# A fused attention and two-layer kernel: the first batch's w1/w2 products ordered by feature tile, its softmax weights transposed by products with a diagonal of reciprocal sums, and more filling products at the start

## The chip, the cores and the metric

The kernel runs as one program on one core of a Trainium2 chip. The metric is the device time of one execution in microseconds (us); a lower number is better. TensorE (called PE in the profile, its weight loads PEld) multiplies, VectorE (DVE) and ScalarE (ACT) do the elementwise work, GpSimd (POOL) issues the loads and stores, and SyncE (SP) issues the transposing transfers of the attention weights.

## The reference, cut to what matters

```python
def _attn_ref(q, k, v):                       # (4, 8, 576, 64), block-causal, block of 64
    scores = scale * np.matmul(q, k.transpose(0, 1, 3, 2))
    scores = np.where(mask, scores, -1000000000.0)
    scores = scores - np.max(scores, axis=-1, keepdims=True)
    attn = np.exp(scores)
    attn = attn / (np.sum(attn, axis=-1, keepdims=True) + 1e-09)
    return np.matmul(attn, v)

def _moe_ref(x, w1, w2, w3, w_out):           # x: 2304 x 512, w1, w2: 512 x 1024
    a = x @ w1
    b = x @ w2
    h = a * b @ w3
    return h @ w_out

def _moe2_ref(x, w_in, w_out):                # 512 -> 2048 -> 512
    h = x @ w_in
    r = np.maximum(h, 0.0)
    return (r * r) @ w_out
```

The attention of 4 batches with 8 heads gives the 2304 x 512 matrix x of the first layer, whose result is the x of the second. The weights come as 64-bit floating-point words.

## The kernel before, in words

**Attention.** The 32 heads are handled as 16 pairs p; pairs 0 to 3 are batch 0, pairs 4 to 7 batch 1, and so on. The 576 queries of a head are cut into five tiles, in three groups g. For each pair and group PE makes the scores `s`, DVE takes the maxima `nm`, ACT makes the exponentials `pf` and their sums `ssum`, and DVE makes the reciprocals `r`. Batch 0 then goes its own way (`whole(p)`): DVE multiplies each row of `pf` by its reciprocal (L842), PE transposes `pf` with the identity `ident` into PSUM (`transpose`, tile `tp`, L900), ACT copies that to `pt` (L906), and PE multiplies `pt` by the values (`attend_whole`, L1003). A group has five transpositions for each of the two heads, so a pair has 30 and the four pairs 120. From batch 1 on ACT and DVE write f16 high and low parts `p`, a DMA transposes them, and PE makes the value products at L949. The result x of a pair is kept as f16 high and low parts in two token parts, x0 (320 tokens) and x1 (256 tokens); g = 0 and g = 1 of the first layer are these two parts.

**Weights.** `w3 @ w_out` is computed once, by the products `po` of `setup_rows` (L1040, evicted by ACT at L1116 and by DVE at L1121). The eight tiles of w1 and w2 (one for 128 features, f = 0 to 7) are converted by `w12_tile`: a load, two passes of ACT and two of DVE, a sum of squares or a maximum, a small product with ones on PE (L351, `wsum`), a scale, and a split into f16 high parts (ACT, L278) and low parts (DVE, L281).

**First layer.** `first_block(b, g)` runs over the eight features f and the two halves `which` (0 for w1, 1 for w2): twelve products `ab` into a PSUM bank, then an eviction by ACT (`a`), a product of both halves by DVE (L1184) and a split into high and low parts of the tile `g`. After all eight features come the products `y` with `w3 @ w_out`, stored to DRAM. The calls for g = 0 and g = 1 follow each other, so that g = 0 wants all eight converted tiles before anything of g = 1 is done. Everything else of PE after that, the rest of the batches and the second layer, follows in the same manner.

**What sets the order.** The program is written as operations with inputs, outputs, an assumed cost and a key; `Order.emit` puts them into each engine's queue: whenever an engine is free in its model, the ready operation with the lowest key comes next. Engines run their queues in order. The keys around the change are these:

```python
key = 2 * p * HEAD + 5 * g          # scores of pair p, group g (HEAD = 10); + 3 behind the softmax
key = (2 * p + 1) * HEAD + 6 + part # value products of pair p
K12 + K12S * (n - 13)               # the 16 half tiles of w1/w2: 60, 62, ... 90 before
```

The products `po`, `ab` and `y` have keys far above these, in the order in which they are written, so they fill PE whenever no attention is ready. For pairs from 4 on, `spare(p)` adds a reserve (2.0 us in the model) before PE's score and value products are thought ready. `Order.idle` calls `warm_up` while the first weights are still on their way: wherever PE would sit idle, it writes filling products `warm_out` (128 columns, bf16) that nobody reads; `begin_warm` and `end_warm` bound that time.

Of the kernel before, what the change touches and what calls it, by code (L numbers as in the profile page):

```python
# [7 lines left out]
F32 = mybir.dt.float32  # L8
# [162 lines left out]
def fused_kernel(ctx: ExitStack, tc: tile.TileContext, qT, kT, vp, va, w12, w3t, wo, wb, out):  # L171
# [45 lines left out]
    GATE_A = 1  # L217
    GATE_G = 1
    KWO, KWOS, KW3, KW3S = 0,3,14,4
    K12 = 60.0  # L220
    K12S = 2.0
    VSL = 7
    LOADL = 2
    VSB = 4.2
# [1 line left out]
    X0KEY = 2.0  # L226

    SPARE = 2.0
    S_SPARE = 0.7


# [261 lines left out]

    def spare(p):

        return SPARE if p >= KDM else 0.0

    raws = {}
    vals = {}
# [18 lines left out]
    table = buf("at", "table", 1, [P, 1], F32, "table")  # L518
    warm_out = buf("p0", "po", 1, [P, 512], F32, "warm_out")

    def warm_up(gap):
        for _ in range(int((0.8 * gap - 0.2) / 0.11)):
            pe.matmul(warm_out()[:, :P], warm(), warm(), start=True, stop=True)

    def begin_warm():
# [199 lines left out]
    def pair(p):  # L725
# [6 lines left out]
        for g, ts_ in enumerate(GROUPS):  # L732
# [101 lines left out]

            od.op(DVE, 0.17, reciprocals, [(ssum, k, a) for k in range(nt) for a in range(2)], [(r,)], key)
            blocks = sum(2 * t + 1 for t in ts_)
            for a in range(2):
                if whole(p):
                    for k, t in enumerate(ts_):
                        od.op(  # L840
                            DVE, 0.12 + 0.0006 * n_keys(t),
                            lambda a=a, k=k, w=weights, r=r: dve.tensor_scalar(  # L842
                                out=w(a, k), in0=w(a, k), scalar1=r()[:, k, a : a + 1], scalar2=None, op0=ALU.mult
                            ),
                            [(r,)], [(pfs[a], k)], key,
                        )
                    transpose(p, g, a, pfs[a], weights, key)
                    continue
                pt = pts[2 * p + a, g] = at_buf(f"pt{g}{a}", 1, [P, blocks, P], F16, f"pt_{name}_{a}")
                pts_of[pt] = 2 * p + a, g  # L850
                p16 = at_buf("p16", P_BUFS, [P, 9 * P], F16, f"p16_{name}_{a}")
                for k, t in enumerate(ts_):
                    nk = n_keys(t)
                    o = PT_BASE[t] * P
                    od.op(
                        ACT, c_act(nk, 0.09),
                        lambda o=o, nk=nk, a=a, k=k, w=weights, p16=p16, r=r: act.activation(  # L857
                            p16()[:, o : o + nk], w(a, k), AF.Copy, scale=r()[:, k, a : a + 1]
                        ),
                        [(pfs[a], k), (r,)], [(p16, "h", t)], key,  # L860
                    )
                    od.op(
                        DVE, c_dve(nk, 0.06),
                        lambda o=o, nk=nk, a=a, k=k, w=weights, p16=p16, r=r: dve.scalar_tensor_tensor(  # L864
                            out=p16()[:, o + nk : o + 2 * nk], in0=w(a, k), scalar=r()[:, k, a : a + 1],
                            in1=p16()[:, o : o + nk], op0=ALU.mult, op1=ALU.subtract,
                        ),
                        [(pfs[a], k), (r,), (p16, "h", t)], [(p16, "l", t)], key,
                    )
                whole_p = [(p16, x, t) for x in "hl" for t in ts_]  # L870
                pt_keys[2 * p + a, g] = [(pt,)]
                od.op(
                    SQ, (1.25, 0.22 * blocks, LATE),
                    lambda p16=p16, pt=pt, blocks=blocks: sp.dma_start_transpose(
                        out=pt(), in_=p16()[:, : blocks * P]
                    ),
                    whole_p, [(pt,), ("pt", 2 * p + a, g)], key,
                )
# [1 line left out]

    WHOLE_PT = {1: (0, 3), 2: (1, 4), 3: (0, 3), 0: (3, 4), 4: (0, 4)}

    def transpose(p, g, a, pf, weights, key):

        ts_ = GROUPS[g]
        name = f"{p}_{g}_{a}"
# [4 lines left out]
        for part, (todo, n) in enumerate(((mains, P), (lasts, 64))):  # L891
# [4 lines left out]
            def go(todo=todo, n=n, tp=tp, first=first):  # L896
                for k, c, o in todo:
                    nq = 64 if ts_[k] == 0 else P
                    at = (o - first) * P
                    pe.transpose(tp()[:n, at : at + nq], weights(a, k)[:nq, c * P : c * P + n], ident()[:nq, :nq])  # L900

            od.op(PE, len(todo) * 0.12 + 0.05, go, [(pf, k) for k in range(len(ts_))] + [(ident,)], [(tp,)], key)
            last = ("pt", 2 * p + a, g)
            od.op(
                ACT, c_act(wide),
# [233 lines left out]

    last_y = []  # L1140

    def first_block(b, g):
        gt0, gn = GS[g]
        x = xs[b, g]
        gs = []
        gt = {}
        for f in range(KFF):
            accs = []
            for which in range(2):
                acc = Acc(gn, f"ab_{b}_{g}_{f}_{which}")  # L1150
                mms = []
                for kc in range(KDM):
                    for a, xn in PRODS:
                        o = which * 512 + kc * P
                        mms.append((
                            lambda a=a, xn=xn, o=o, kc=kc, f=f: (w12_view(f, a)[:, o : o + P], x[xn][kc]()),
                            [w12_key(f, a, which), (x[xn][kc],)],
                        ))
                accumulate(acc, mms, gn, next_key(), c_mm16)
                accs.append(acc)  # L1160
                back = Part(ab_back[b], 2 * f + which, 1)
                if which == 0:
                    av = buf("mo1", "a", 2, [P, GMAX], F32, f"a_{b}_{g}_{f}")
                    od.op(
                        ACT, c_act(gn, 0.09),
                        lambda av=av, acc=acc, back=back: act.activation(av()[:, :gn], acc(), AF.Copy, scale=back()),
                        [acc.key, (ab_back[b], f)], [(av,)], K_EVICT,
                    )
                else:
                    if f % 4 == 0:  # L1170
                        gt[f // 4] = g_buf(f // 4, f"g_{b}_{g}_{f}")
                    t = gt[f // 4]
                    o = 2 * (f % 4)

                    def hi(t=t, o=o):
                        return t()[:, o * GMAX : o * GMAX + gn]

                    def lo(t=t, o=o):
                        return t()[:, (o + 1) * GMAX : (o + 1) * GMAX + gn]

                    kh, kl = (t, "h", f % 4), (t, "l", f % 4)
                    od.op(
                        DVE, c_dve(gn, 0.06),
                        lambda acc=acc, av=av, back=back: dve.scalar_tensor_tensor(  # L1184
                            out=av()[:, :gn], in0=acc(), scalar=back(), in1=av()[:, :gn], op0=ALU.mult, op1=ALU.mult
                        ),
                        [acc.key, (ab_back[b], f)], [(av,)], K_EVICT,
                    )
                    split(hi, lo, lambda av=av: av()[:, :gn], gn, ([kh], [kl], (av,)), K_EVICT)
                    gs.append(((hi, lo), (kh, kl)))  # L1190

        def ys_products(key=None):
            for e in range(KDM):
# [680 lines left out]
    for b in range(B):  # L1874
# [22 lines left out]
            begin_blocks()  # L1897
        else:
            ab_scales(b)
        for g in range(2):  # L1900
            first_block(b, g)
    second_block()
    od.emit()

# [50 lines left out]
```

## Time and profile before

| | |
|---|---|
| median of 3 runs | 885.81 us (885.78 to 887.76) |
| profiled execution | 883.62 us, of which the span of its instructions is 881.5 us |
| PE busy in the span | 850.7 us (97%), 7143 products |
| DVE, ACT, POOL busy | 632.6 us (72%), 571.7 us (65%), 107.9 us (12%) |
| mean granted TensorE clock | 0.988 of full speed |

The profile is one execution. Times in its rows are microseconds from the start of the span; an engine's idle time in a stretch is the stretch less its busy time. The granted clock has two levels here, 1.2 and 2.4 GHz, shown as 0.5 and 1.0 of full speed.

### The profile page before, as it was taken

The numbers are of one execution on the slowest core, as the hardware profiler recorded it, in microseconds if no ns is written. First come the engines' busy times: TensorE is split into PE (matmuls) and PEld (weight loads), VectorE is DVE, ScalarE is ACT, GpSimd is POOL, SyncE is SP. The second block draws the span as 40 slices with busy tenths as digits, with TensorE's granted clock in tenths as the row PEclk, the third lists the DMA queues.
The fourth block names the chain that finished last, engine by engine and source line by source line (L and its number), as shares of the span: only waits on it lengthen the run. The fifth ranks groups of instructions, "written<-read, shape, count | busy, mean of one in ns | idle before, by whom it ended". The sixth has DMA issues, their size and how long they took to land.

```text
span 881.5 us, 18383 instructions
## 1 busy us (share of the span) xinstructions
PE 850.7 (97%) x7143; PEld 643.7 (73%) x7147; DVE 632.6 (72%) x1470; ACT 571.7 (65%) x1304; POOL 107.9 (12%) x202
## 2 busy tenths in 40 slices
PE   7799988899999999999999999999999999999998
PEld 6477875588877888779979877666666666666664
DVE  5987979888778787763993788997853474375443
ACT  5987878677766676774895696664544464464343
POOL 5111112020121101002221111000010000000000
PEclk8999998899999999999999999999999999999999
DMA  8833348589998999883563342000020002001001
GB/s 312 321 123 104 122 147 231 125 149 185 183 196 158 184 167 177 155 136 111 195 204 119 105 143 73 1 25 1 2 97 1 1 29 67 1 1 48 1 1 48
DMA packets 104247, 98.06 MB, mean 111 GB/s; under 512 B 82976, under 2 KB 86816, under 8 KB 102752
## 3 DMA queue, kind: packets, MB, share of 16 engines
q0 software_dynamic: 17568, 69.09, 24.6%
q1 hardware_dynamic: 86592, 27.80, 18.9%
q8 instruction: 56, 0.92, 0.4%
q14 instruction: 31, 0.25, 0.1%
HBM read 60.69 MB, written 9.44 MB: 80 GB/s over the span
## 4 chain that ended last, share of the span: by engine, by line
PE 59%; DVE 3%; ACT 1%; issue 0%; DVEq 0%
PE o L1785 20%; PE p L1721 16%; PE ab L1040 11%; PE y L1040 7%; PE h L1636 2%; PE pv_bank L949 1%; PE s L757 1%; PE ny L1343 0%; DVE s L1663 0%; DVE nm L791 0%; DVE g L271 0%; DVE ob L1795 0%; DVE c L1742 0%; DVE p L864 0%; PE nq L1464 0%
## 5 line engine op out<-in xcount | busy, mean ns | idle before, releaser
L1785 PE MATMUL o<-wb,g 128*128 128x512 f16 x864 | 194.5, 379 | 0.1
L1040 PEld LDWEIGHTS <-w 128*128 128x128 f16 x1536 | 147.8, 99 | 51.8 <-ACT w L278 4.7
L1785 PEld LDWEIGHTS <-g 128*128 128x128 f16 x864 | 84.0, 98 | 92.4 <-issue 0.6
L1040 PE MATMUL ab<-x0h,w 128*128 128x320 f16 x512 | 112.8, 307 | 6.8 <-ACT w L278 3.1
L1040 PE MATMUL y<-g,w3o 128*128 128x320 f32 (+1 forms) x768 | 110.1, 299 | 0.5 <-DVE g L242 0.5
L816 ACT ACTIVATE pf<-s,nm 128x192 f32<-128x192 f32 (+4 forms) x160 | 82.9, 527 | 39.6 <-DVE nm L799 39.5
L1040 PEld LDWEIGHTS y<-g,w3o 128*128 128x128 f32 x768 | 103.6, 188 | 3.8 <-issue 1.9
L1609 ACT ACTIVATE c<-c,beta 128x512 f32<-128x512 f32 x64 | 45.4, 713 | 81.5 <-DVE c L1742 81.4
L1040 PE MATMUL ab<-x1h,w 128*128 128x256 f16 x512 | 87.9, 273 | 0.5 <-DVE a L1184 0.5
L1721 PEld LDWEIGHTS <-wb 128*128 128x128 f16 x768 | 75.2, 98 | 15.8 <-issue 0.2
L271 DVE TENSOR_TENSOR g<-c,g 128x512 f16<-128x512 f32 x64 | 43.7, 689 | 48.8 <-ACT g L269 48.8
L1040 PE MATMUL ab<-x0l,w 128*128 128x320 f16 x256 | 78.4, 306 | 0.0
L864 DVE SCALAR_TENSOR_TENSOR p<-pf,r,p 128x192 f16<-128x192 f32 (+2 forms) x120 | 62.6, 546 | 16.4 <-ACT p L857 15.7
L1040 PE MATMUL ab<-x1l,w 128*128 128x256 f16 x256 | 69.8, 272 | 0.0
L857 ACT ACTIVATE p<-pf,r 128x192 f16<-128x192 f32 (+2 forms) x120 | 60.8, 559 | 5.0 <-ACT pf L816 1.6
L1040 PE MATMUL po<-wo,w 128*128 128x256 f32 (+1 forms) x360 | 55.5, 303 | 8.6 <-DVE w3o L1121 4.8
L1721 PEld LDWEIGHTS <-st 128*128 128x128 f16 x576 | 56.4, 98 | 7.4
L1742 DVE TENSOR_TENSOR c<-p,x 128x512 f32<-128x512 f32 x32 | 22.1, 690 | 50.9 <-PE p L1721 40.2
L1040 PEld LDWEIGHTS po<-wo,w 128*128 128x128 f32 x360 | 47.1, 195 | 14.0 <-DVE w3o L1121 3.9
L757 PE MATMUL s<-kraw,qraw 64*128 64x288 f32 (+4 forms) x384 | 54.5, 409 | 1.2 <-ACT pf L816 1.2
L332 DVE CUSTOM_DVE_ANT_0 cx<-raw,cx 128x1024 uint16<-128x1024 uint16 (+1 forms) x61 | 47.6, 781 | 2.9 <-ACT raw L323 0.4
L319 ACT ACTIVATE raw<-raw 128x512 f32<-128x512 f32 (+1 forms) x61 | 46.4, 763 | 1.6 <-DMA raw<-in_w 1.4
(213 smaller groups left out, 1645.6 us busy)
## 6 DMA issues: line engine op xcount, KB each, us to landing
raw<-in_wb POOLq DMA_DIRECT2D x32, 512.0 KB, 4.9
raw<-in_w3t POOLq DMA_DIRECT2D x8, 1024.0 KB, 12.6
raw<-in_w POOLq DMA_DIRECT2D x16, 512.0 KB, 5.0
vraw<-in_vp POOLq DMA_DIRECT2D x16, 320.0 KB, 4.9
qraw<-in_qT POOLq DMA_DIRECT2D x16, 288.0 KB, 4.1
kraw<-in_kT POOLq DMA_DIRECT2D x32, 144.0 KB, 4.3
yraw<-ydram POOLq DMA_DIRECT2D x8, 512.0 KB, 4.7
vmix<-v SPq DMA_DIRECT2D x24, 160.0 KB, 4.4
```

The lines of the kernel that those rows point to most:

```text
L271: DVE, c_dve(n), lambda: dve.tensor_tensor(out=lo(), in0=src(), in1=hi(), op=ALU.subtract), kh + ks, kl, key
L319: act.activation(up, up, AF.Prelu, scale=2.0**-112, alpha=2.0**32)
L332: dve.tensor_tensor(out=x(), in0=x(), in1=words()[1], op=ALU.add)
L757: pe.matmul(o[:, h] if t == 4 else o, q()[rows, q_start(t) : q_start(t) + 128], keys_()[rows, c], start=True, stop=True,)
L816: act.activation(o, view(a, t), AF.Exp, bias=nm()[:, k, a : a + 1], scale=SCALE, accum_out=ssum()[:, k, a : a + 1],)
L857: lambda o=o, nk=nk, a=a, k=k, w=weights, p16=p16, r=r: act.activation(p16()[:, o : o + nk], w(a, k), AF.Copy, scale=r()[:, k, a : a + 1]),
L864: lambda o=o, nk=nk, a=a, k=k, w=weights, p16=p16, r=r: dve.scalar_tensor_tensor(out=p16()[:, o + nk : o + 2 * nk], in0=w(a, k), scalar=r( ...
L1040: pe.matmul(acc(), l, r, start=k == 0, stop=k == len(mms) - 1)
L1609: lambda: act.activation(src(), src(), AF.Relu, scale=beta()[:, j, k : k + 1]),
L1721: pe.matmul(acc()[:, TH * half : TH * half + TH], lhs(a, kc), y[yn]()[:, kc], start=n == 0, stop=n == len(mms) - 1,)
L1742: DVE, c_dve(n), lambda: dve.tensor_tensor(out=o(), in0=x(), in1=y(), op=ALU.add), r, w, K_EVICT
L1785: pe.matmul(o(), g[gx]()[:, cols], wt(f)[:, a, 512:1024], start=(begin and n == 0), stop=(last and n == 2),)
```

## The change

Four things are changed.

1. For batch 0 the first layer goes feature tile by feature tile: for each f the products of both token parts, and the products `y` only after all eight. Token part 1 gets `g` tiles of its own (`w8_0`, `w8_1`, where the converted w_out was). The other batches keep their order.
2. In batch 0 the rows of `pf` are no longer multiplied by the reciprocals. DVE makes for each group a tile `dg` of diagonal matrices, the identity times the reciprocals, one for each tile and head, and the transposition becomes an ordinary F32 product of `pf` with its diagonal matrix. The costs that the planner assumes for it are unchanged.
3. The conversions of w1 and w2 get the keys 50, 54, ... 110, and the reserve of pairs 4 to 7 falls from 2.0 to 1.0.
4. `warm_up` counts 0.062 instead of 0.11 us for a filling product after its first use, so that a gap of the same length gets more of them (170 in all instead of 114).

```diff
-    K12 = 60.0
-    K12S = 2.0
+    K12 = 50.0
+    K12S = 4.0
...
+    SPARE_1 = 1.0
...
-        return SPARE if p >= KDM else 0.0
+        return 0.0 if p < KDM else SPARE_1 if p < 2 * KDM else SPARE
...
+    warm_cost = [0.11]
+
     def warm_up(gap):
-        for _ in range(int((0.8 * gap - 0.2) / 0.11)):
+        n = int((0.8 * gap - 0.2) / warm_cost[0])
+        if n > 0:
+            warm_cost[0] = 0.062
+        for _ in range(n):
             pe.matmul(warm_out()[:, :P], warm(), warm(), start=True, stop=True)
...
+            if whole(p):
+                dg = at_buf("dg", 2, [P, 4, P], F32, f"dg_{name}")
+                od.op(
+                    DVE, c_dve(2 * nt * P),
+                    lambda nt=nt, dg=dg, r=r: dve.tensor_tensor(
+                        out=dg()[:, : 2 * nt], in0=ident().unsqueeze(1).broadcast_to([P, 2 * nt, P]),
+                        in1=r().rearrange("p k a -> p (k a)")[:, : 2 * nt].unsqueeze(2).broadcast_to([P, 2 * nt, P]),
+                        op=ALU.mult,
+                    ),
+                    [(r,), (ident,)], [(dg,)], key,
+                )
             for a in range(2):
                 if whole(p):
-                    for k, t in enumerate(ts_):
-                        od.op(
-                            DVE, 0.12 + 0.0006 * n_keys(t),
-                            lambda a=a, k=k, w=weights, r=r: dve.tensor_scalar(
-                                out=w(a, k), in0=w(a, k), scalar1=r()[:, k, a : a + 1], scalar2=None, op0=ALU.mult
-                            ),
-                            [(r,)], [(pfs[a], k)], key,
-                        )
-                    transpose(p, g, a, pfs[a], weights, key)
+                    transpose(p, g, a, pfs[a], weights, dg, key)
...
-                    pe.transpose(tp()[:n, at : at + nq], weights(a, k)[:nq, c * P : c * P + n], ident()[:nq, :nq])
-
-            od.op(PE, len(todo) * 0.12 + 0.05, go, [(pf, k) for k in range(len(ts_))] + [(ident,)], [(tp,)], key)
+                    pe.matmul(
+                        tp()[:n, at : at + nq], weights(a, k)[:nq, c * P : c * P + n], dg()[:nq, 2 * k + a, :nq],
+                        start=True, stop=True,
+                    )
+
+            od.op(PE, len(todo) * 0.12 + 0.05, go, [(pf, k) for k in range(len(ts_))] + [(dg,)], [(tp,)], key)
...
+    def first_block(b):
+        gs = [Products() for _ in GS]
+        if b:
+            for g in range(2):
+                for f in range(KFF):
+                    ab_products(b, g, f, gs[g])
+                y_products(b, g, gs[g])
+            return
+        for f in range(KFF):
+            for g in range(2):
+                ab_products(b, g, f, gs[g])
+        for g in range(2):
+            y_products(b, g, gs[g])
```

The first place is DVE behind the reciprocals `r` of pair 1, group 1 (the names carry pair, group and head). Before:

```order
L829 TENSOR_SCALAR r_1_1_657<-ssum_1_1_617 128x4
L833 RECIPROCAL r_1_1_657<-r_1_1_657 128x4
L842 TENSOR_SCALAR pf_1_1_0_616<-pf_1_1_0_616,r_1_1_657 128x448
L1121 TENSOR_TENSOR w3o_0_532<-po_405,w3o_0_532 128x256
L842 TENSOR_SCALAR pf_1_1_0_616<-pf_1_1_0_616,r_1_1_657 128x64
L842 TENSOR_SCALAR pf_1_1_1_647<-pf_1_1_1_647,r_1_1_657 128x448
L242 TENSOR_TENSOR w3_3_661<-cx_9_600,w3_3_661 128x1024
L842 TENSOR_SCALAR pf_1_1_1_647<-pf_1_1_1_647,r_1_1_657 128x64
```

With the change:

```order
L835 TENSOR_SCALAR r_1_1_685<-ssum_1_1_637 128x4
L839 RECIPROCAL r_1_1_685<-r_1_1_685 128x4
L847 TENSOR_TENSOR dg_1_1_694<-ident_92,r_1_1_685 128x512
L330 TENSOR_SCALAR cx_9_697<-raw_9_200 128x1024
L780 MEMSET s_1_2_0_688 64x64
```

Four passes over `pf` have become one over `dg`, and both heads' products wait for that one.

The second place is PE at the transpositions of pair 1, group 0, with the products `po` between the two heads. Before:

```order
L900 MATMUL tp_1_0_0_0_595<-ident_92,pf_1_0_0_538 128x128 x3
L900 MATMUL tp_1_0_0_1_603<-ident_92,pf_1_0_0_538 64x128 x2
L1040 MATMUL po_405<-wo_1_417,w3_1_535 128x256 x6
L900 MATMUL tp_1_0_1_0_619<-ident_92,pf_1_0_1_545 128x128 x3
L900 MATMUL tp_1_0_1_1_623<-ident_92,pf_1_0_1_545 64x128 x2
```

With the change:

```order
L909 MATMUL tp_1_0_0_0_599<-dg_1_0_594,pf_1_0_0_558 128x128 x3
L909 MATMUL tp_1_0_0_1_604<-dg_1_0_594,pf_1_0_0_558 64x128 x2
L1052 MATMUL po_459<-wo_0_307,w3_1_587 128x256 x6
L1052 MATMUL po_459<-wo_1_468,w3_1_587 128x256 x6
L1052 MATMUL po_459<-wo_2_522,w3_1_587 128x256 x6
L909 MATMUL tp_1_0_1_0_639<-dg_1_0_594,pf_1_0_1_583 128x128 x3
L909 MATMUL tp_1_0_1_1_646<-dg_1_0_594,pf_1_0_1_583 64x128 x2
```

The number of products in the program is the same; their second operand is the diagonal matrix.

The third place is PE at the end of the first feature tile of token part 0 of batch 0 (`ab_` is followed by batch, token part, feature and half). Before:

```order
L1040 MATMUL ab_0_0_0_1_1650<-x0h3_0_1345,w12_0_1224 128x320
L1040 LDWEIGHTS w12_0_1224
L1040 MATMUL ab_0_0_0_1_1650<-x0l3_0_1355,w12_0_1224 128x320
L1040 LDWEIGHTS w12_0_1224
L1040 MATMUL ab_0_0_0_1_1650<-x0h3_0_1345,w12_0_1224 128x320
L1040 LDWEIGHTS w12_0_1224
L1040 MATMUL ab_0_0_1_0_1674<-x0h0_0_468,w12_0_1224 128x320
```

With the change:

```order
L1052 MATMUL ab_0_0_0_1_1717<-x0l3_0_1465,w12_0_1184 128x320
L1052 LDWEIGHTS w12_0_1184
L1052 MATMUL ab_0_0_0_1_1717<-x0h3_0_1455,w12_0_1184 128x320
L352 LDWEIGHTS ones_90
L352 MATMUL pv_bank_281<-wsum_3_1662,ones_90 128x2
L1052 LDWEIGHTS w12_0_1184
L1052 MATMUL ab_0_1_0_0_1742<-x1h0_0_596,w12_0_1184 128x256
```

After tile 0 of token part 0 now come tile 0 of token part 1 and the small product of tile 3, where tile 1 of token part 0 stood. The score products of pair 4's last group have moved ahead of tile 0, and those of pair 5 ahead of the small product of tile 7, behind which they stood.

## Rows read from the trace of the kernel before

**Rows 1.** The page: busy time, share, instructions; then the clock in 40 slices.

```profile
PE 850.7 (97%) x7143; PEld 643.7 (73%) x7147; DVE 632.6 (72%) x1470; ACT 571.7 (65%) x1304; POOL 107.9 (12%) x202
...
PEclk8999998899999999999999999999999999999999
```

**Rows 2.** Stretches: length, busy time (count) of each engine, clock, DMA share, GB/s.

```profile
13.00:46.50 33.50, 26.05 (x183) 18.67 (x183) 30.69 (x59) 32.25 (x60) 5.44 (x9) 0.91 0.87 332
46.50:113.00 66.50, 64.71 (x545) 54.15 (x543) 56.58 (x137) 54.29 (x134) 11.31 (x21) 0.97 0.36 119
113.00:130.30 17.30, 13.30 (x118) 11.79 (x118) 13.01 (x37) 13.13 (x34) 1.58 (x3) 1.00 0.50 158
130.30:166.00 35.70, 28.84 (x173) 17.88 (x173) 33.01 (x92) 28.21 (x65) 6.47 (x12) 0.86 0.66 179
166.00:300.00 134.00, 132.24 (x1409) 108.89 (x1408) 108.33 (x287) 93.99 (x269) 21.13 (x39) 1.00 0.91 172
300.00:881.00 581.00, 576.60 (x4631) 423.91 (x4633) 385.31 (x850) 346.43 (x739) 51.94 (x94) 1.00 0.30 76
```

**Rows 3.** What PE waited for from 113 to 170: total, times, longest.

```profile
PE ab L1040 <- ACT w L278: 3.1, 2, 2.1
PE ab L1040 <- DVE w L281: 2.7, 3, 1.0
PE po L1040 <- ACT w3o L1116: 1.8, 2, 1.3
```

**Rows 4.** The stretches at half clock behind 46 us, same columns as rows 2.

```profile
46.55:49.97 3.42, 3.42 (x18) 3.42 (x18) 3.35 (x11) 2.76 (x3) 0.00 (x0) 0.50 0.56 237
148.95:155.78 6.83, 5.99 (x24) 3.46 (x25) 5.51 (x15) 3.97 (x7) 0.53 (x1) 0.50 0.88 198
162.61:166.02 3.41, 3.20 (x13) 1.78 (x14) 3.17 (x9) 2.86 (x7) 0.00 (x0) 0.50 0.51 141
```

**Rows 5.** Loads of PE in order of time: start, length, count.

```profile
66.64 0.50 PEld L900 LDWEIGHTS tp<-ident,pf 128*128 128x128 f32 x5
67.14 0.30 PEld L1040 LDWEIGHTS po<-wo,w 128*128 128x128 f32 x2
...
137.37 0.30 PEld L605 LDWEIGHTS pv_bank<-vdiag,ones 128*128 128x128 f32 x2 [0.46 <-DVE vdiag L599]
137.59 0.21 PEld L1040 LDWEIGHTS <-w 128*128 128x128 f16 x2
```

**Rows 6.** The transpositions by stretch: busy time (count) of PE, PEld, ACT.

```profile
13.00:46.50 33.50, 5.77 (x30) 3.68 (x30) 4.38 (x12) 0.91 0.87 332
46.50:113.00 66.50, 13.81 (x90) 9.35 (x90) 12.45 (x34) 0.97 0.36 119
```

**Rows 7.** DVE's instructions at L842 and L242: ns min/median/max, first and last start, forms.

```profile
L842 DVE TENSOR_SCALAR pf<-pf,r x40: 244/379/522, 12.7 to 107.3; 128x192 f32<-128x192 f32 x8, 128x320 f32<-128x320 f32 x8, 128x448 f32<-128x448 f32 x8, 128x64 f32<-128x64 f32 x8
...
L242 DVE TENSOR_TENSOR g<-a,g x64: 395/443/493, 135.4 to 508.6; 128x320 fp32r<-128x320 f32 x32, 128x256 fp32r<-128x256 f32 x32
...
L242 DVE TENSOR_TENSOR wo<-cx,wo x5: 691/1199/1226, 17.8 to 37.1; 128x1024 fp32r<-128x1024 f32 x3, 128x512 fp32r<-128x512 f32 x2
```

**Rows 8.** PE in order of time near 137 and 145: 54 products between both starts.

```profile
137.70 0.30 PE L1040 MATMUL ab<-x0h,w 128*128 128x320 f16 x1
...
144.90 0.30 PE L1040 MATMUL ab<-x0h,w 128*128 128x320 f16 x1
```

**Rows 9.** DVE's low parts of w1/w2: the tile at 116 and the eighth.

```profile
116.12 1.41 DVE L281 SCALAR_TENSOR_TENSOR w<-cx,wsc,w 128x512 f16<-128x512 f32 x2
...
169.83 0.75 DVE L281 SCALAR_TENSOR_TENSOR w<-cx,wsc,w 128x512 f16<-128x512 f32 x1
```

**Rows 10.** PE from 13 to 21 us in order of time.

```profile
13.20 1.32 PE L900 MATMUL tp<-ident,pf 128*128 128x128 f32 x5 [3.23 <-DVE pf L842]
...
15.95 3.69 PE L523 MATMUL warm_out<-warm 128*128 128x128 bf16 x35
...
20.73 1.23 PE L757 MATMUL s<-kraw,qraw 64*128 64x288 f32 x6 [0.40 <-ACT pf L816]
```

More of the change, by code (lines that the diff above doesn't have):

```diff
@@ L881, in fused_kernel, with transpose @@
     WHOLE_PT = {1: (0, 3), 2: (1, 4), 3: (0, 3), 0: (3, 4), 4: (0, 4)}
-    def transpose(p, g, a, pf, weights, key):
+    def transpose(p, g, a, pf, weights, dg, key):
         ts_ = GROUPS[g]
@@ L1140, in fused_kernel @@
     last_y = []
-    def first_block(b, g):
-        gt0, gn = GS[g]
[L1144 to L1190, printed above, removed]
@@ new lines, in g_at @@
+    def g_at(b, g, f, gs):
+        gn = GS[g][1]
+        wide = GMAX if b or not g else gn
+        m = f % 4
+        if not m:
+            name = f"g_{b}_{g}_{f}"
+            if b or not g:
+                gs.tiles.append(g_buf(f // 4, name))
+            else:
+                gs.tiles.append(buf("base", f"w8_{f // 4}", 1, [P, 8 * gn], F32R, name))
+        t = gs.tiles[f // 4]
+        return (
+            lambda: t()[:, 2 * m * wide : 2 * m * wide + gn],
+            lambda: t()[:, (2 * m + 1) * wide : (2 * m + 1) * wide + gn],
+            (t, "h", m), (t, "l", m),
+        )
@@ new lines, in fused_kernel, with __init__, ab_products @@
+    class Products(list):
+        def __init__(self):
+            self.tiles = []
+    def ab_products(b, g, f, gs):
+        gn = GS[g][1]
+        x = xs[b, g]
+        av = buf("mo1", "a", 2, [P, GMAX], F32, f"a_{b}_{g}_{f}")
+        for which in range(2):
+            acc = Acc(gn, f"ab_{b}_{g}_{f}_{which}")
+            mms = []
+            for kc in range(KDM):
+                for a, xn in PRODS:
+                    o = which * 512 + kc * P
+                    mms.append((
+                        lambda a=a, xn=xn, o=o, kc=kc: (w12_view(f, a)[:, o : o + P], x[xn][kc]()),
+                        [w12_key(f, a, which), (x[xn][kc],)],
+                    ))
+            accumulate(acc, mms, gn, next_key(), c_mm16)
+            back = Part(ab_back[b], 2 * f + which, 1)
+            if which == 0:
+                od.op(
+                    ACT, c_act(gn, 0.09),
+                    lambda acc=acc, back=back: act.activation(av()[:, :gn], acc(), AF.Copy, scale=back()),
+                    [acc.key, (ab_back[b], f)], [(av,)], K_EVICT,
+                )
+                continue
+            hi, lo, kh, kl = g_at(b, g, f, gs)
+            od.op(
+                DVE, c_dve(gn, 0.06),
+                lambda acc=acc, back=back: dve.scalar_tensor_tensor(
+                    out=av()[:, :gn], in0=acc(), scalar=back(), in1=av()[:, :gn], op0=ALU.mult, op1=ALU.mult
+                ),
+                [acc.key, (ab_back[b], f)], [(av,)], K_EVICT,
+            )
+            split(hi, lo, lambda: av()[:, :gn], gn, ([kh], [kl], (av,)), K_EVICT)
+            gs.append(((hi, lo), (kh, kl)))
@@ L1192, in ys_products, with y_products @@
+    def first_block(b):
[11 more added lines that the diff above has]
+            y_products(b, g, gs[g])
+    def y_products(b, g, gs):
+        gt0, gn = GS[g]
         def ys_products(key=None):
@@ L1899, in fused_kernel @@
             ab_scales(b)
-        for g in range(2):
-            first_block(b, g)
+        first_block(b)
     second_block()
```

## The prediction

> **What bounds the kernel now.** I read the page first: PE is busy for 97% of the span and no other engine for more than 72% [rows 1], so the time is PE's work, plus PE's idle time, plus what it loses at half clock. The clock line says that all of that loss lies early; the table of stretches then says where the idle time is [rows 2]. PE idles 7.4 us of the 33.5 between 13 and 46.5, 1.8 of the 66.5 to 113, 4.0 of the 17.3 to 130.3, 6.9 of the 35.7 to 166, 1.8 of the 134 to 300, and 4.4 of the 581 behind that. So from 166 on there is nothing to win, and whatever PE has finished earlier or later there shifts the end by as much. The stage to read is 113 to 166: there the waits of PE name the conversions of w1/w2 (L278, L281) and the evictions of w3 times w_out (L1116) [rows 3], that is, DVE and ACT are behind. DVE is busy 33.0 of the 35.7 us from 130.3 on [rows 2]. Behind two of these waits the clock falls to half for 6.83 and 3.41 us [rows 4]; PE is busy 5.99 and 3.20 us there, work that takes half as long at full clock, so 4.6 us are lost. Idle and clock together cost 4.0 + 6.9 + 4.6 = 15.5 us in this stage. Another 1.7 us (half of 3.42) go at 46.55 [rows 4].
>
> **The diagonal products.** This part adds work to PE. Five transpositions in a row take 0.50 us until the next load, 0.10 each; the only ordinary F32 product of 128 by 128 with 128 columns (L605) takes two loads and 0.22 us until the next one [rows 5]. The program has the same 120 products, each now of that kind: 0.12 us more by these rows, 0.10 if a product is just two transpositions long. I take 0.11, since eight products are only 64 wide and some loads overlap. 30 of them lie before 46.5 and 90 behind it [rows 6]. The 90 stand where PE is busy 64.7 of 66.5 us, so they cost in full: 90 x 0.11 = 9.9 us. The 30 add 3.3 us to a stretch in which PE idles 7.4 us and DVE (30.7) and ACT (32.3 of 33.5) set the pace [rows 2]; they lie beside that.
>
> DVE loses 40 passes of 0.379 us on average, 15.2 us, and gets 12 passes over `dg`. A product of two operands with 512 elements takes 0.691 us, one with 256 the 0.395 at the lower end of the `g` row [rows 7]: 8 x 0.69 + 4 x 0.40 = 7.1 us. No row has an operand that is one value repeated 128 times; the bounds are the 1.2 us of the 1024-wide row (12 us in all) and the 0.244 us of the cheapest pass (3 us). I take 7.1. DVE so has 8.1 us less to do before 113, about 2.5 of them before 46.5; this costs and gains nothing by itself but lets the conversions come earlier, and PE's idle time from 13 to 46.5 shrink. For that stretch I take a gain of 1 us, between 2 and a loss of 3.3 (all 30 products on the path). If the pause before 46.55 shrinks, the half clock there goes too: 1.0 of its 1.7 us, between none and all.
>
> Behind the wait for `dg` stand both heads' products, and behind them ACT's copies in its queue; before, a head waited for two passes over `pf` (0.76 us), now both wait for one (0.69). So that wait is not longer.
>
> **Feature tile by feature tile.** 54 products of 320 columns take 7.2 us between the starts at 137.70 and 144.90 (53 steps), 0.136 each [rows 8]; with 256 columns by proportion 0.109. A converted tile so gave PE 24 x 0.136 = 3.3 us of work before, and gives 24 x (0.136 + 0.109) = 5.9 now. The conversions deliver a tile every 9 us: from the tile at 116.1 to the eighth at 169.8 there are six steps [rows 9]. Before, PE wanted eight tiles in 26 us, hence the waits. Now I follow PE: it came to tile 0 at 130.3; 9.9 later, less 1 and 1 for the early part, less the 4.0 of idle time before 130.3 (DVE has 8.1 us less to do and PE comes later, so w3's evictions are done), makes 134. Add 1.2 for the scores of pair 4 moved ahead (moved, not new) and six tiles of 5.9 with the scores of pair 5 (3.3) and the small products (0.8): PE wants tile 6 at 175 and tile 7, after another 5.9 and pair 4's value products and scores (5), at 186. Before the change the eighth tile was written at 170.6 [rows 9]. In return ACT and DVE must evict token part 1 within the same time: on DVE the `g` row's 0.40 and about as much for the product ahead of it, 0.8 us a tile, 6 us up to the eighth, less than the 8.1 saved. With 10 us to spare the waits of 130 to 166 and their half clock should go. I take 14.0 of the 15.5 us, leaving 1.5 for round trips.
>
> **Keys and reserve.** The new keys bring tile 0 forward and spread the last ones among pairs 4 and 5; that is in the margin above. The reserve of 1.0 lets PE come to pairs 4 to 7 earlier. PE idles 1.8 us in 166 to 300 [rows 2]; I add 0.5, between 0 and 8 (rival 1).
>
> **Filling products.** 35 of them took 3.69 us at half clock, 0.105 each [rows 10]; 66 take as long at full clock, and 25 more ahead of 13.20 take 1.3 to 2.6 of the 3.23 us that PE waited there. If the clock stays low, the 66 end 3.3 us later, at about 23, and the scores behind them, which had to wait for ACT until 20.73 anyway [rows 10], lose 2 us; ACT has conversions of w_out to do meanwhile. Nothing, or 1 us in the bound above.
>
> **The sum.** +9.9 - 1.0 - 1.0 - 14.0 + 0.5 = -5.6 us. Against the profiled execution (883.62) that is 878.0; the median of the runs, 885.81, is 2.2 above that one execution, and I set the sum against the median: 880.2, so 880.
>
> **The rivals.** Rival 1, slower: the place is the score and value products of pairs 4 to 7, between 166 and 260. With 1.0 us of reserve instead of 2.0, each of their 16 groups can find its data up to 1 us late, 16 us in all. The DMA engines, which transpose these pairs' weights, are 91% busy there; against it, PE hardly waits there now [rows 2]. It decides from 5.6 us of such waits on; half of them, 8 us, give 888.2, and with a fall of the clock 890. Rival 2, no change: the conversions don't profit. ACT loses no work, is busy 28.2 of 35.7 us there [rows 2], and takes on token part 1; if the tiles slip by 16 us against my count, PE waits for some 6 of them and the gain is gone: 885.8. Rival 3, a larger gain: the whole 15.5 and the 1.7 go, and the early stretch gains 4 of its 7.4 us because DVE is lighter from the first pair on: 9.9 - 15.5 - 1.7 - 4 = -11.3, 874.5. Rival 4: an ordinary F32 product costs four transpositions instead of two: 0.40 us against 0.10, 0.30 more for each of the 120; of the first 30 (9.0 us) 1.6 stick out of the idle 7.4, the 90 cost 27, less 16 for the other terms is 12.6 slower: 898.4. The trace speaks against it, since the 0.22 us of L605 are just twice the 0.10 to 0.11 [rows 5].
>
> The Trainium skill, TensorE: Matmul & The Clock Gate, section Terms, calls the transposing mode four times faster for FP32, which speaks for rival 4 and against this change. By that rule the sum would be that of rival 4, by the row it is the -5.6 above; the two products of L605 are the nearest row, and they decide.
>
> **The numbers.** Chances: the forecast 0.56 (by itself 877 to 883), rival 1 0.12, rival 2 0.16, rival 3 0.13, rival 4 0.03. The range leaves out rivals 1 and 4 and the lower end of rival 3: 873 to 888. A measurement of this kernel tells 0.3%, some 2.7 us, from no change. Faster by more: forecast and rival 3, less a little at 883, 0.67; within: rival 2 and that little, 0.17; slower: rivals 1 and 4 and an edge of rival 2, 0.16.
>
> **What would show it.** 240 products into `tp` for 120, their loads 0.11 apart; 12 passes over `dg` near 0.69 and 0.40; from 46.5 to 113 no more idle time, but PE reaching the first `ab` some 4 us later; then, up to the first `y`, hardly a wait on L278 or L281 and full clock; behind that the same stretch as before, some 6 us earlier. I am wrong if the products into `tp` cost more than 0.13 each, if waits on the conversions stay, or if waits on pairs 4 to 7 appear.

## The result, and the profile after

The changed kernel takes 894.80 us (median of 4 runs, 893.97 to 895.32) where the kernel before took 885.90 beside it (4 runs, 885.78 to 887.76): a ratio of 1.0103, 95% interval 1.0069 to 1.0137. It is slower; I had forecast 880.0. The profiled execution took 893.97 us with a span of 892.2, 10.7 longer than before.

The page: busy time, share and count of each engine, and the clock in 40 slices, beside [rows 1].

```profile
PE 866.6 (97%) x7323; PEld 657.7 (74%) x7323; DVE 628.6 (70%) x1442; ACT 572.4 (64%) x1304; POOL 107.7 (12%) x202
...
PEclk9999999999999999999999999999999999999999
```

PE is busy 15.9 us more, and its idle time is 25.6 us (892.2 - 866.6) instead of 30.8: the change took away waits and half clock, as meant, and put more work in their place than it took. The stretches, with the columns of [rows 2], show where:

```profile
13.00:46.50 33.50, 28.58 (x241) 21.40 (x242) 29.38 (x54) 30.42 (x58) 4.97 (x9) 1.00 0.82 323
46.50:113.00 66.50, 62.27 (x512) 51.74 (x511) 43.61 (x94) 48.43 (x114) 8.08 (x15) 1.00 0.31 100
113.00:130.30 17.30, 17.30 (x141) 14.12 (x140) 12.59 (x31) 12.66 (x29) 3.83 (x7) 1.00 0.51 163
130.30:166.00 35.70, 31.42 (x263) 25.17 (x262) 31.27 (x89) 28.06 (x70) 7.01 (x13) 1.00 0.61 166
166.00:300.00 134.00, 128.95 (x1359) 103.54 (x1359) 111.73 (x291) 97.30 (x268) 21.15 (x39) 1.00 0.88 172
```

These stretches no longer hold the same work, so I also compared the traces at equal work: I added up PE's products in order of their starts, weighted by columns and without those into `tp` and `warm_out`, and looked when the changed kernel had started as much as the kernel before had at a given moment. The difference is the lag; the other columns are differences in PE's busy time for `tp`, in its idle time, and the rest (fillers, half clock) up to that point.

```
before at    after at    lag    tp     idle   rest
 46.5          48.2     +1.7   +4.7   -4.5   +1.5
130           144.0    +14.0  +15.8   -3.5   +1.7
170           174.8     +4.8  +15.8   -7.6   -3.4
230           239.4     +9.4  +15.8   -4.2   -2.2
end                    +10.7  +15.8   -5.2   +0.1
```

Each lag compares one execution with one other. The profiled execution of the kernel before (883.62) lies 2.3 us below its median here, so by the medians the end is +8.9 and not +10.7.

The products into `tp` by stretch, busy time of PE, PEld and ACT in that order (30 and 90 of them in [rows 6], in all 19.58 us; two of the 240 lie across 46.5 and are counted twice), then the new passes of DVE:

```profile
0.00:46.50 46.50, 9.99 (x68) 7.93 (x69) 4.81 (x12) 1.00 0.79 296
46.50:150.00 103.50, 25.36 (x174) 19.74 (x172) 14.12 (x36) 1.00 0.37 115
...
L847 DVE TENSOR_TENSOR dg<-ident,r x12: 424/691/693, 13.3 to 125.5; 128x512 f32<-128x512 f32 x8, 128x256 f32<-128x256 f32 x4
```

PE's waits over the whole span (total, times, longest), then those from 113 to 170 beside [rows 3], then those from 170 to 300:

```profile
PE po L1052 <- DVE w3o L1133: 3.9, 6, 0.9
PE tp L909 <- DVE dg L847: 3.4, 2, 2.3
PE po L1052 <- ACT w3o L1128: 2.6, 4, 1.2
...
PE po L1052 <- ACT w3o L1128: 1.6, 2, 1.2
PE pv_bank L352 <- ACT junk L408: 0.9, 1, 0.9
...
PE pv_bank L611 <- DVE x1l L977: 1.4, 1, 1.4
PE pv_bank L352 <- ACT g L240: 1.4, 1, 1.4
PE pv_bank L352 <- DVE wsum L401: 1.0, 1, 1.0
PE pv_bank L961 <- DVE x0l L977: 0.6, 1, 0.6
```

PE no longer waits for converted tiles of w1/w2 (L278 and L281 before), and the half clock has gone. But the waits on w3's evictions stayed, and small new ones stand between 170 and 230, where there had been hardly any: 1.4 and 1.0 us at the small products with ones that belong to the conversions (`wsum`, L352), 1.4 and 0.6 us behind the low parts of the attention's result (`x1l`, `x0l`).

### The profile page after: what moved, and what is told of

Same layout as the page of the kernel before. It is cut to its first block, busy times and chain, and to the rows that moved or that the text cites. A ratio compares the mean times of both kernels' runs of the same rounds, so it can differ in the third digit from the quotient of the medians.

```text
span 892.2 us, 18705 instructions
## 1 busy us (share of the span) xinstructions
PE 866.6 (97%) x7323; PEld 657.7 (74%) x7323; DVE 628.6 (70%) x1442; ACT 572.4 (64%) x1304; POOL 107.7 (12%) x202
## 4 chain that ended last, share of the span: by engine, by line
PE 46%; DVE 6%; ACT 4%; issue 1%; DVEq 0%; ACTq 0%
PE o L1820 20%; PE p L1756 15%; PE y L1052 4%; PE ab L1052 4%; PE h L1671 2%; DVE cx L333 1%; ACT wb L279 1%; DVE wb L282 1%; DVE a L1202 1%; ACT pf L822 1%; DVE cx L330 1%; PE ny L1378 0%; ACT p L866 0%; DVE p L873 0%; ACT a L1195 0%
## 5 line engine op out<-in xcount | busy, mean ns | idle before, releaser
L1052 PE MATMUL ab<-x0h,w 128*128 128x320 f16 x512 | 109.5, 299 | 0.6 <-DVE w3o L1133 0.6
L1052 PE MATMUL ab<-x0l,w 128*128 128x320 f16 x256 | 76.5, 299 | 0.0
L763 PE MATMUL s<-kraw,qraw 64*128 64x288 f32 (+4 forms) x384 | 56.5, 413 | 0.3 <-ACT pf L822 0.2
L763 PEld LDWEIGHTS s<-kraw,qraw 64*128 64x128 f32 x384 | 34.9, 188 | 16.1 <-issue 8.8
```

The lines of the kernel that those rows point to most:

```text
L763: pe.matmul(o[:, h] if t == 4 else o, q()[rows, q_start(t) : q_start(t) + 128], keys_()[rows, c], start=True, stop=True,)
L1052: pe.matmul(acc(), l, r, start=k == 0, stop=k == len(mms) - 1)
```

## The experiments

My first theory (T1) was that the diagonal products alone cost more than I had counted. The rivals were a planner misled by their old price (T2) and the keys and the reserve (T3); later runs brought theory P, on the pace of the second batch's attention. Times are device microseconds. The kernel before ran beside each group at 884.4 (e1 to e4), 884.9 (e5 to e8 and e9 to e11) and 885.9 (e12 to e14), so the ratios are what compares.

**e1, everything but the diagonal products.** The scaling passes and the transpositions of before come back:

```diff
-                    pe.matmul(tp()[:n, at : at + nq], weights(a, k)[...], dg()[:nq, 2 * k + a, :nq], ...)
+                    pe.transpose(tp()[:n, at : at + nq], weights(a, k)[...], ident()[:nq, :nq])
```

> The changed kernel with the transpositions by the identity and the 40 passes over pf put back; order by feature tile, keys, reserve and filling products stay. Theory 1 (price of the products: in the trace a group of five takes PE 1.45 us to the next load against 0.55 before, of which 0.3 us are pauses where the weights change between 128 and 64 columns): the 0.9 us of some 18 to 24 groups fall away, 16 to 21 us, less what waits come back: 874 to 881 us. Theory 2 (the planner still counts 0.12 us a product, so that ACT's copies are queued too early): its costs are right again for the identity, 876 to 882 us, not told from theory 1 here. Theory 3 (keys and reserve do the harm): 890 to 895 us.

Measured: 888.78, ratio 1.0037 (1.0009 to 1.0065). T1 missed: without the diagonal products the change is still slower than before. Its lag is -3.7 us at 170, so order, keys and fillers do gain there, and +3.7 at 210. Rows of ACT, then of PE, from its trace:

```profile
191.65 0.78 ACT L863 ACTIVATE p<-pf,r 128x576 f16<-128x576 f32 x1
196.29 0.77 ACT L863 ACTIVATE p<-pf,r 128x576 f16<-128x576 f32 x1 [3.86 <-DMA pt<-p]
196.97 0.51 ACT L1189 ACTIVATE a<-ab,ab_back 128x320 f32<-128x320 f32 x1
...
197.53 0.27 PE L1046 MATMUL ab<-x1h,w 128*128 128x256 f16 x1 [1.10 <-ACT a L1189]
202.04 4.37 PE L1046 MATMUL y<-g,w3o 128*128 128x320 f32 x15 [3.03 <-DVE a L1196]
```

ACT waits for a DMA that transposes weights of the second batch. Behind that wait in its queue stands the eviction of `ab`, and for that PE waits. The attention of pairs 4 to 7 has come between PE and its products.

**e2, the diagonal products alone.** The kernel before, with the second part of the change only (the same lines the other way).

> The kernel before with the diagonal products alone. Theory 1: 16 to 21 us more work on PE, of which the waits of PE between 113 and 166 us hide up to 8: 893 to 902 us. Theory 2: waits rather than work, 889 to 895 us. Theory 3: no harm without the keys, 883 to 888 us.

Measured: 904.01, ratio 1.0215 (1.0164 to 1.0266). Near T1, a little above its 893 to 902, and further above what T2 and T3 gave. The lag is +18.4 at 120, with 16.9 us more in `tp`, and +22.4 at 300.

**e3, all weights 128 wide.** The loads of 64 columns take the 64 keys ahead of them along, and ACT copies the lower half:

```diff
+            def last(a, k, pfs=pfs, offs=offs, ts_=ts_):
+                o = offs[k] + ts_[k] * P - 64
+                return pfs[a]()[:, o : o + P]
...
-                        tp()[:n, at : at + nq], weights(a, k)[:nq, c * P : c * P + n], dg()[:nq, 2 * k + a, :nq],
+                        tp()[:, at : at + P], weights(a, k)[:, c * P : c * P + P] if n == P else last_of(a, k),
+                        dg()[:, 2 * k + a],
```

> The changed kernel with all weights of the diagonal products 128 columns and rows wide: for the last 64 keys of a tile the 64 keys ahead of them are taken along, and ACT copies partitions 64 to 127. Theory 1: no change of width within a group and to the next products of 128 columns, a group takes 1.1 to 1.2 us instead of 1.45, 0.3 us x 18 to 24 groups: 887 to 890 us. Theory 2 and theory 3: no more than 1 us from 894.8.

Measured: 890.62, ratio 1.0068 (1.0044 to 1.0093): by the ratios 3.1 us less than the whole change, a little less than T1 wanted. Loads of PE in order of time (start, length, count), a group of five products and the load behind it, first of the changed kernel (the second row is the end of the first), then of e3, then e3's `tp` in a stretch:

```profile
71.30 1.29 PEld L909 LDWEIGHTS tp<-dg,pf 128*128 128x128 f32 x10
72.40 0.19 PEld L909 LDWEIGHTS tp<-dg,pf 128*64 128x64 f32 x2
72.76 0.41 PEld L1052 LDWEIGHTS po<-wo,w 128*128 128x128 f32 x3 [0.17 <-issue]
```

```profile
71.55 1.21 PEld L912 LDWEIGHTS tp<-dg,pf 128*128 128x128 f32 x10
72.67 0.43 PEld L1056 LDWEIGHTS po<-wo,w 128*128 128x128 f32 x3
...
46.50:150.00 103.50, 23.87 (x180) 21.63 (x180) 15.31 (x36) 1.00 0.42 125
```

With equal widths a group lasts 72.67 - 71.55 = 1.12 us, ten passes of 0.11; with a 64-wide product at its end 72.76 - 71.30 = 1.46. Changing the width costs PE some 0.2 us each way, and that goes when the widths are equal. In `tp` it comes to 25.36 - 23.87 = 1.5 us behind 46.5, and over the whole span to 35.35 - 31.97 = 3.4.

**e4, the products' true price in the planner's table.**

```diff
-            od.op(PE, len(todo) * 0.12 + 0.05, go, ...
+            od.op(PE, len(todo) * 0.222 + 0.3, go, ...
```

> The changed kernel with the planner told what the trace shows of the diagonal products (0.222 us each and 0.3 us a group part instead of 0.12 and 0.05). Theory 1: the work stays, 892 to 896 us. Theory 2: ACT no longer waits for the products (10.9 us in the trace), PE no longer for the evictions (6.5 us): 884 to 889 us. Theory 3: no change, 893 to 896 us.

Measured: 894.36, ratio 1.0101 (1.0051 to 1.0150). T2 falls.

**e5, the order alone; e6 to e8, one more part of e1 undone each.**

```diff
-    K12 = 50.0          # e5 and e7: 60.0 and 2.0 again
-    K12S = 4.0
-    SPARE_1 = 1.0       # e5 and e6: 2.0
-            warm_cost[0] = 0.062    # e5 and e8: 0.11
```

> Only the new order of the first batch (feature tile by feature tile) is left of the change; transpositions, keys, reserve and fillers are those of before. Theory A (the keys and the reserve lost the gain, the order is good): the waits of 130 to 166 on the conversions and their half clock go, some 7 to 12 us, and nothing is given back in 170 to 230: 874 to 880. Theory B (the order itself moves the attention of the second batch later and behind the evictions of both token parts, so ACT and DVE stand still there whatever the keys): the gain is given back as in the run without the diagonal products, 886 to 891, with waits of PE on a or y between 190 and 215.

> The changed kernel with the old transpositions and the old reserve of 2.0 for pairs 4 to 7; the new keys stay. The run with reserve 1.0 gave 888.8 where the kernel before gave 884.4. Theory A, if the reserve is to blame: the 7.4 us lost around 195 to 213 shrink to 2 or less, 880 to 884. If the keys are to blame, or theory B: 887 to 891.

> The changed kernel with the old transpositions and the old keys of the conversions (60 and 2); the reserve of 1.0 stays. Theory A, if the keys are to blame: pairs 4 and 5 are less delayed by conversions, the loss around 195 to 213 shrinks, 880 to 885. If the reserve is to blame, or theory B: 887 to 891.

> The changed kernel with the old transpositions and the old number of filling products. If the fillers are neutral, as I predicted: within 1.5 us of the same kernel with them (888.8), 887 to 890. Rival: they keep the clock up between 12 and 19 us and win what the half clock cost there; without them half clock from 12.4 to 19.3 returns and the time is 2 to 4 us longer, 891 to 893.

Measured: e5 889.58, ratio 1.0039 (1.0022 to 1.0057); e6 882.94, 0.9976 (0.9959 to 0.9993); e7 884.22, 0.9987 (0.9970 to 1.0004); e8 886.97, 1.0013 (0.9996 to 1.0030). Against e1 (1.0037), taking back the reserve helps, taking back the keys helps, and taking back both and the fillers does not: neither is the cause by itself, and theory A falls. Why two steps help alone and not together was not found. B's outcome came in e5, but not as B said: nothing is lost between 190 and 215. Its lag is -12.2 us at 170, almost what I had forecast for the order; it is still -10.2 at 242, and -0.9 at 260. There PE stands still for 6.1 us, and the clock falls to 0.89 on average (stretch 225 to 255 of the kernel before with the last value products of its pair 7, then of e5):

```profile
225.00:255.00 30.00, 30.00 (x326) 24.99 (x321) 23.92 (x58) 20.15 (x58) 7.05 (x14) 1.00 1.10 216
...
243.71 0.97 PE L949 MATMUL pv_bank<-pt,v 128*64 128x128 f16 x28
```

```profile
225.00:255.00 30.00, 23.87 (x272) 16.98 (x272) 20.68 (x50) 18.79 (x49) 5.82 (x11) 0.89 1.12 196
...
225.90 0.31 PE L1046 MATMUL ab<-x0h,w 128*128 128x320 f16 x1
...
230.46 2.05 PE L763 MATMUL s<-kraw,qraw 64*128 64x192 f32 x16
236.03 0.75 PE L763 MATMUL s<-kraw,qraw 64*128 64x288 f32 x2 [3.52 <-ACT pf L822]
238.88 2.29 PE L763 MATMUL s<-kraw,qraw 64*128 64x288 f32 x6 [2.09 <-ACT pf L822]
241.09 0.85 PE L955 MATMUL pv_bank<-pt,v 128*64 128x256 f16 x8
...
247.77 0.97 PE L955 MATMUL pv_bank<-pt,v 128*64 128x128 f16 x28
...
236.89 0.63 ACT L822 ACTIVATE pf<-s,nm 128x448 f32<-128x448 f32 x1 [0.91 <-DVE nm L805]
```

PE is through with the first batch at 225.9 (before: 242.8) and begins the second batch's `ab` on pairs 4 to 6. Then it needs `x0` of pair 7, whose value products come at 241.09, and has only scores left, which wait for ACT, and ACT waits for DVE's row maxima (8.0 us from 215 to 242; before, 3.8). The last value products of pair 7 start at 247.77; in the kernel before at 243.71, where PE had work of the first batch to 242.7. Theory P: the attention of the second batch has a pace of its own, and the store of first-batch products just covers it.

**e9 and e10, the second batch's attention made lighter.** Pairs 4 to 7 leave out the row maximum (a zero stands in its place), on e5 and on the kernel before:

```diff
+            if KDM <= p < 2 * KDM:
+                od.op(
+                    DVE, 0.12, lambda nm=nm, nt=nt: dve.memset(nm()[:, :nt], 0.0),
+                    [], [(nm, k, a) for k in range(nt) for a in range(2)], key,
+                )
             for k, t in enumerate(ts_):
+                if KDM <= p < 2 * KDM:
+                    continue
```

> The kernel before with the new order alone (889.6 us with the same order and nothing left out), where pairs 4 to 7 leave out the reduction to the row maximum (a zero stands in its place): 24 passes of DVE fewer between 170 and 245, 16.2 us, on the way from scores to weights. Theory P (the second batch's attention has a pace of its own, set by ACT, DVE and the transposing DMAs, and ends at 244 to 248 however early PE is; the gain of the order waits for it at 230 to 250): the last value product of pair 7 comes at 235 or earlier instead of 247.8, the idle time and half clock of 230 to 250 shrink by most of their 7.6 us, and the time falls to 876 to 882. Rival Q (the planner's order of PE itself is to blame, whatever the pace): 886 to 890, the waits only change their names.

> The kernel before, with the same reductions left out in pairs 4 to 7. Theory P: here PE still has products of the first batch until 242.7, so attention that is ready earlier gains nothing: within 2 us of the kernel before. Rival Q, or if DVE's load by itself limits this stretch: 3 or more faster.

Measured: e9 874.75, ratio 0.9878 (0.9848 to 0.9908); e10 881.81, 0.9971 (0.9944 to 0.9997). The same relief is worth 3.1 us on the kernel before and 14.8 on the new order. Both are more than P gave: e9 lies below its 876 to 882, and the 3.1 are past the 2 us that P allowed and at the 3 from which Q, or the load of DVE by itself, was to show. That the new order gains 11.7 us more is what P says and Q does not. e9's stretch:

```profile
225.00:255.00 30.00, 28.50 (x285) 22.07 (x285) 20.77 (x50) 20.90 (x60) 4.90 (x9) 1.00 0.93 180
```

PE is busy 28.50 of 30 us instead of 23.87, and the lag stays: -9.3 at 170, -6.6 at 260, -8.0 at the end. One number missed: pair 7's value products came at 234.7 and 244.7, where I had expected the last by 235; what counts for PE is the first of them, 6.4 earlier than in e5. Leaving out operations also makes the planner place the others anew, so the 14.8 us are not the maxima alone; no run lightened the attention in an unchanged order.

**e11, the whole change with the old reserve; e12, the whole change without the maxima of pairs 4 to 7; e13, e6 with a reserve of 4.0; e14, the kernel before with the new fillers alone.** The edits are lines shown above, for e14 those of the diff on `warm_cost`.

> The whole change, but with the old reserve of 2.0 for pairs 4 to 7. Without the diagonal products the same step took 5.9 us off. Theory P: pairs 4 to 7 already run late here (value products of pair 7 to 259 instead of 244) and the reserve moves them by little; I expect 889 to 894, so that the cost of the diagonal products alone leaves it slower than before. If the reserve is a cause of its own: 886 to 889.

> The whole change (894.8 us), with the row maximum left out in pairs 4 to 7 (a zero in its place). Theory P: of the 10.7 us by which its trace is behind at the end, 4.6 were lost between 170 and 230, where the second batch's attention came last, and 1 to 2 behind 400; with that attention faster, these come back, and what stays is what the diagonal products cost less the gain of the order, +4.8 at 170: 886 to 890. Rival D (the price of the diagonal products is all, the pace plays no part in the whole change): 892 to 895.

> New order, new keys, more fillers, old transpositions, with a reserve of 4.0 for pairs 4 to 7 where 2.0 gave 882.9 and 1.0 gave 888.8. Theory P: a larger reserve puts more products of the first batch between scores and value products, but the attention keeps its pace and the store of such products is as large as before; it helps by 2 us at most: 880 to 884. If the reserve by itself sets the loss: another 3 to 6 off, 877 to 880.

> The kernel before with the larger number of filling products alone. As I predicted: within 1 us of the kernel before. Rival: full clock from 12 to 19 us brings the scores of the first pair 1 to 3 us earlier, and the time falls by as much.

Measured: e11 893.78, ratio 1.0097 (1.0070 to 1.0124); e12 890.21, 1.0051 (1.0029 to 1.0073); e13 890.62, 1.0046 (1.0027 to 1.0066); e14 882.71, 0.9980 (0.9958 to 1.0002). In the whole change the reserve is not the cause (e11). e12 is 4.6 us below the whole change, at the upper edge of what P expected and outside D (its lag is +3.7 at 170, +6.4 at 230, +7.1 at the end). But the same step takes 3.1 us off the kernel before (e10), so only 1.5 are left for the change itself, and the intervals are wider than that: what share of its loss the pace of the second batch has is not shown. e13 missed both theories: a reserve of 4.0 is worse than 2.0 (e6). Its stretch, then rows of PE, DVE and ACT:

```profile
225.00:255.00 30.00, 21.76 (x237) 17.10 (x237) 19.02 (x53) 19.65 (x63) 7.05 (x13) 0.89 0.79 177
...
221.77 10.47 PE L1046 MATMUL y<-g,w3o 128*128 128x256 f32 x86
232.17 1.24 PE L763 MATMUL s<-kraw,qraw 64*128 64x288 f32 x8
...
233.49 0.18 DVE L780 MEMSET s<- 64x64 f32 x2 [2.02 <-PE s L763]
...
234.54 0.53 ACT L966 ACTIVATE x0h<-pv_bank,vback 128x320 f16<-128x320 f32 x1 [2.97 <-PE pv_bank L955]
```

PE idles even longer there than in e5, and the last value products of pair 7 start at 260.8. Ahead of that it works through 86 products `y` in one piece, while DVE (2.0 us) and ACT (3.0 us) stand still for scores and value products that come behind them in PE's queue. For these 2 to 3 us the second batch waits for the order of PE and not for its own pace, which P has no place for; the rest of the delay of pair 7 (17 us against the kernel before) was not followed. The kernels side by side, lags against the kernel before:

```
                          lag at 170   pair 7's last at   lag at 260   lag at end
before                         0            243.7              0            0
e5 order                     -12.2          247.8            -0.9         +4.2
e6 + keys, fillers            -8.0          247.4            -0.4         -1.2
e1 + reserve 1.0              -3.7          253.9            +3.8         +5.3
e13 reserve 4.0               -5.2          260.8           +10.5         +8.5
e9 e5 without maxima          -9.3          244.7            -6.6         -8.0
after                         +4.8          259.3            +9.1        +10.7
e2 diagonal alone            +15.5          262.4           +19.4        +22.6
```

Among the kernels with the new order, the lag at 260 goes with pair 7's last value products, whatever it was at 170; only e9, where that attention is lighter, keeps its lead. What sets the time of pair 7 is not settled by this: it lies between 244.7 and 260.8 in these kernels, so it is no fixed pace, and the planner's placing has a part in it (e13). The last column is of single executions; by the medians e13 ends at +4.8 and e2 at +19.7. With nothing left out, the fastest is e6 (or e14, which can't be told from no change): 0.24% below the kernel before, within the 0.3% that a measurement here can tell.

## Why the prediction was wrong

The sum of -5.6 us became +10.7 in span (+8.9 by the medians). By its own steps, with the lags of the table above (stage up to 46.5, to 130, to 170, to the end):

- **Early stretch, -1.0 forecast, +1.7 measured.** The 30 early products did lie beside the idle time (+4.7 in `tp`, -4.5 idle); the gain of 1 us on top did not come, and the 56 more fillers, counted as nothing, are 1.5 us of PE. Whether these cost anything is not settled: without them e1 became 2.1 us faster by the ratios (e8), with them the kernel before became no slower (e14).
- **46.5 to 130, +4.9 forecast (9.9 for the products, -1.0 for half clock, -4.0 for idle time), +12.3 measured.** The 90 products cost 25.36 - 13.81 = 11.5 us by stretch (11.1 at equal work), some 0.13 each instead of 0.11; two loads of 0.11 were right, the changes of weight width were missing. The larger part is a step that failed: "less the 4.0 of idle time before 130.3 (DVE has 8.1 us less to do and PE comes later, so w3's evictions are done)". The idle time up to there changed by +1.0 instead, and the first `ab` came at 145.91 where the prediction had 134. PE's waits on `w3o` before (the 2.7 lie ahead of 46.5) and after, where two totals stand above, with one row of each:

```profile
PE po L1040 <- DVE w3o L1121: 4.8, 6, 2.7
PE po L1040 <- ACT w3o L1116: 2.3, 3, 1.3
PE ab L1040 <- DVE w3o L1121: 1.0, 1, 1.0
...
127.58 1.69 PE L1040 MATMUL po<-wo,w 128*128 128x256 f32 x12 [0.59 <-DVE w3o L1121]
```

```profile
PE ab L1052 <- DVE w3o L1133: 0.6, 1, 0.6
...
143.13 0.98 PE L1052 MATMUL po<-wo,w 128*128 128x256 f32 x6 [0.59 <-DVE w3o L1133]
```

  Behind 46.5 PE waits 7.1 us in all for `w3o` (3.9, 2.6 and 0.6) where it waited 5.4 (8.1 less the 2.7): DVE with fewer passes over `pf` (its whole busy time fell by 4.0 us) did not shorten these waits. Lengths of 0.47 behind ACT and 0.59 behind DVE come back in both traces, beside shorter and longer ones (0.29 to 1.33). The lengths that come back look like a round trip from product to eviction to product and not like an engine that is behind; no run took them away, so the cause of these waits stays open. A full clock saved nothing that can be seen up to here.
- **130 to 170, -10.0 forecast, -9.2 measured.** This step held: no waits on L279 and L282, full clock, and e5 gives the order alone -12.2 at 170.
- **Behind 170, +0.5 forecast, +5.9 measured.** "So from 166 on there is nothing to win, and whatever PE has finished earlier or later there shifts the end by as much" is the step that failed, and the main one, since the change without the diagonal products gains nothing either (e1). PE does not idle there in the kernel before, which has a store of first-batch products beside the second batch's attention. Taking PE through that store earlier did not bring the attention earlier: e5 lost 11.3 of its 12.2 us between 170 and 260, where pair 7's last value products came at 247.8 instead of 243.7. That e9 keeps its lead speaks for the attention as the bound there; why it is ready when it is stays open (e13). The whole change lost 4.6 up to 230, and of its 4.8 us of waits there 2.4 are at the small products of the conversions and 2.0 behind the attention's result, so that its loss has this same cause is not shown. Rival 1 had the place (pairs 4 to 7) in part and about the size, but not the cause: it blamed the reserve, and e11 clears it for the whole change; without the diagonal products 2.0 was better than 1.0 (e6), and 4.0 was not (e13).

The four deviations, 2.7 + 7.4 + 0.8 + 5.4, make the 16.3 us between forecast and trace. The two halves of the change do not add up: the diagonal products alone cost 19 us (e2), and the rest of the change takes some 10 off that and nothing off the kernel before (e1). It would follow from the same if a PE that is late by 15 us has attention to catch up with, and a PE that is early waits for it; that is argued and not shown. Why e2 loses another 6 us between 250 and 300 was not followed to its end.

Rival 4 is out: a product is two passes of 0.11 us and a transposition one. The Trainium skill, TensorE: Matmul & The Clock Gate, section Terms, has the transposing mode four times faster for FP32; the traces here show twice, and the pauses besides.

## What to carry to other kernels

An engine that does not idle in a stretch may be covering a chain beside it: before counting a gain through to the end, look at when that chain (here pair 7's value products, at 243.7, one microsecond behind the last first-batch product) would be ready if the cover came earlier. Take part of the chain's work away in a run that leaves something out, on the old and on the new version: if the new one gains much more (here 14.8 us against 3.1), the chain is likely the bound, as far as the order of the rest stays the same. And when a wait keeps its length though the engine it names gets lighter, look for another cause than that engine's load before counting the wait as saved.

## What was not expected of the hardware

In these traces, ordinary F32 products whose weights change between 128 and 64 columns lose some 0.2 us of PE at each change: the load behind comes 0.31 us after the last instead of 0.11, and with equal widths the step is 0.11 throughout (1.12 us for the group instead of 1.46). The transposing form of before ran five such loads, 64-wide ones among them, in 0.50 us [rows 5]. The pass that multiplies an operand of one value repeated 128 times costs DVE the same here as the shortest ordinary one of 512 elements in [rows 7], 0.691 us; with 256 elements it took 0.424, where the shortest ordinary one took 0.395.
